# Sliding-window attention and soft-MoE slots on one core: the end of the kernel with direct products of the last weight chunks, and with 5/4 of an expert's second half held back instead

## The chip, the cores and the metric

The kernel runs on one core of one Trainium2 chip. The metric is the device time of one execution in microseconds; lower is better. The median of three runs is shown, and next to it the profile of one execution.

## The reference, and what is computed

Attention over 8 batches x 8 heads x 576 tokens with 64 values a head. Heads 0 to 3 see a window of 32 tokens back, heads 4 to 7 every fourth token of the last 128. Its output, 4608 tokens x 512 values (x), goes into a mixture of experts with 8 experts and 4 slots each:

```python
logits = x @ phi                                  # 4608 x 32
d = np.exp(logits - logits.max(0, keepdims=True))
d /= d.sum(0, keepdims=True) + 1e-09
slot_input = (d.T @ x).reshape(8, 4, 512)
for e in range(8):
    slot_out[e] = np.maximum(slot_input[e] @ w1[e], 0.0) @ w2[e]
c = np.exp(logits - logits.max(1, keepdims=True))
c /= c.sum(1, keepdims=True) + 1e-09
return c @ slot_out.reshape(32, 512)              # 4608 x 512, float32
```

w1 is 8 x 512 x 1024 and w2 is 8 x 1024 x 512. All inputs are float32.

## The kernel before, in words

The program is first a list of operations, each with its engine, a cost, a key and what it reads and writes (`Prog.op`). `Prog.schedule` then plans them: whenever an engine is free, it takes the operation that can start earliest by the costs and the planned landings of loads, and among those within 0.12 us of each other the one with the lowest key. What comes out is a fixed order for each engine. The instructions of SP and POOL keep the order of the program text. `Prog.emit` writes the orders out, with semaphore waits where one engine depends on another. So the orders are settled before the run, and a late operand holds up whatever stands behind it on that engine. In one stretch of the plan (`FILL`) idle time of PE is filled with matmuls whose results nobody reads (L1052, "fillers").

Attention runs in eight units. POOL issues the loads: for each unit q, k and v, and between them the weights, which are cast from float32 to bf16 on the way. PE transposes, makes scores and products, ACT takes exponentials, DVE masks and normalises. For each batch the logits give expT (32 slots spread over 128 rows, times the tokens), and the slot inputs are summed up in a PSUM bank.

After the last unit, with keys from K1 on, comes the stage around the change:

- The slot inputs go through w1 (L814) and a ReLU, give h_sb, and are transposed into hT (L832, L841). `rsum` (L852) sums expT per token, and rtok is its reciprocal.
- `ffn2` (L893) multiplies with w2: for each expert it makes matmuls over chunks cc of the 1024 hidden values, eight chunks an expert, into one of two PSUM banks `sp_[h_]`, one for each half of the 512 output columns ("first half" is columns 0 to 255). Four experts stand side by side in 32 columns of PE each. All calls of `ffn2` are tied into one chain, in the order of the text (`chain`, L891).
- `half(h_, key)` (L939) finishes one half of the columns. The bank is scaled with rcs and becomes so_sb; products of expT with so_sb give the rows of the output, which ACT or DVE scale with rtok on the way from PSUM to SBUF and SP stores (`store`, L920).

The last loads that POOL issues are w25, then, for each half of the columns, expert 6 (512 KB), expert 7 without its last two chunks (384 KB) and the last two chunks alone (128 KB). After them come 15 loads of a few bytes each into a tensor that nothing reads (L782).

The last two chunks of expert 7 (cc 6 and 7) are treated apart. Before `half`, h_sb's columns of those chunks are scaled with m7, which keeps expert 7's rows alone (L863 to L874), and multiplied with the first 512 tokens of expT; that gives two tiles G (L877, evicted on L881 and L884). In `half` so_sb is made without the two chunks. The first two sets of 256 tokens are then the sum of a product with so_sb (L957) and of two *direct* products, of G with the weights of the chunks (L960). Only then does `ffn2((7,), 6, 8, ...)` (L969) complete the bank. All other rows use so_all, a second copy: POOL copies its rows 0 to 95 from so_sb (L944), and the rows 96 to 127, where expert 7 stands, are scaled from the complete bank (L977). The sets o = 2 to 5 of the half use it (L989).

`NAB` is 6: six sets of 256 tokens are stored half by half, 256 KB each. The other 3072 tokens follow when both halves are there, in full rows, as groups of 4, 4, 8 and 8 rows for each partition (L1021 on; products on L1034; evictions by `scaled`, L931 on DVE and L932 on ACT; stores of 1, 1, 2 and 2 MB).

Around the change: `wload` on L773 to L777, `NAB` and `GRP` on L844 and L845, lines 863 to 885, `chain` on L891, `half` from L939, the calls of `ffn2` on L1009 to L1017, and the groups on L1020 and L1021.

Of the kernel before, what the change touches and what calls it, by code (L numbers as in the profile page):

```python
# [302 lines left out]
def bass_dilated_sliding_attn__then__soft_moe_slots_kernel(  # L303
# [46 lines left out]
    so_fin = psA_sb[:].bitcast(BF16)[:, 0:DM]  # L350
    m7 = sb("m7", [128, 1], F32)
# [47 lines left out]
    b_m7 = Buf()  # L399
# [374 lines left out]
    for h_ in range(2):  # L774
        sl = (256 * h_, 256 * h_ + 256)
        wload("w26", ((0, 8) + sl,))
        wload("w27", ((0, 6) + sl, (6, 8) + sl))  # L777

    mk = sb("mk", [15, 136])
    for n_ in range(1, 16):  # L780
        o_ = sum(range(n_))
        op("pool", lambda g, n_=n_, o_=o_: [g.dma_start(mk[0:n_, o_:o_ + n_], moe_w2[7, 0:n_, 0:n_])],  # L782
           cost=0.3, sem=DmaSem(nc, f"s_mark{n_}"), nbytes=1024)
# [60 lines left out]
    NAB = 6  # L844
    GRP = [2] * NAB + [4, 4, 8, 8]  # L845
    rs = tile(psum, 1)

    def rsum(t):
# [13 lines left out]
    op("dve", lambda vv: vv.tensor_reduce(m7[:], ident[:, 100:104], mybir.AxisListType.X, AluOp.add),  # L862
       r=[b_id], w=[b_m7], cost=0.1, key=K1)  # L863
    op("dve", lambda vv: vv.tensor_tensor(m7[:], m7[:], rcs[:], AluOp.mult),
       r=[b_rcs], w=[b_m7], cost=0.1, key=K1)
    h7 = tile(pPT)
    G = [tile(pPT), tile(pPT)]

    def so_all(p0=0, p1=128, sl=slice(0, 512)):
        return so_fin[p0:p1, sl]  # L870
    op("dve", lambda vv: vv.tensor_scalar(sbt(h7)[:, 0:256].rearrange("p (f c) -> p f c", c=2),
                                          h_sb[:].rearrange("p (f c) -> p f c", c=8)[:, :, 6:8],
                                          m7[:, 0:1], None, op0=AluOp.mult),
       r=[b_m7] + b_h, w=[h7], alloc=[h7], cost=0.3, key=K1 + 1.5)  # L874
    for c in range(2):
        gp = tile(psum, 1)
        op("pe", lambda t, c=c, gp=gp: t.matmul(bank(gp)[:, 0:NG], sbt(h7)[:, c:256:2], expT[:, 0:NG],  # L877
                                                start=True, stop=True),
           r=[h7] + b_expT[:2], w=[gp], alloc=[gp, G[c]], cost=0.25, key=K1 + 1.6)
        if c == 0:  # L880
            op("act", lambda ac, gp=gp: ac.activation(sbt(G[0])[:, 0:NG], bank(gp)[:, 0:NG], ACTF.Copy),  # L881
               r=[gp], w=[G[0]], cost=0.6, key=K1 + 1.7)
        else:
            op("dve", lambda vv, gp=gp: vv.tensor_copy(sbt(G[1])[:, 0:NG], bank(gp)[:, 0:NG]),  # L884
               r=[gp], w=[G[1]], cost=0.6, key=K1 + 1.7)

# [4 lines left out]
    chain = []  # L891

    def ffn2(es_, lo, hi_, h_, key, after=()):  # L893
# [3 lines left out]
        def pe(t):  # L897
            for cc in range(lo, hi_):
# [8 lines left out]
               a=[sp_[h_], b_sp[h_]], cost=0.12 * (hi_ - lo), mode="c", key=key, after=chain[-1:] + list(after))  # L907
        chain.append(o)
# [11 lines left out]
    def store(d0, n, ap, ob, key, h_=None):  # L920
        so = DmaSem(nc, f"s_out{d0}_{h_}")
        s_out.append(so)
        dst = out[d0:d0 + 128 * n, :].rearrange("(p j) f -> p j f", j=n)
        if h_ is not None:
            dst, ap = dst[:, :, CH[h_]], ap[:, :, CH[h_]]
        op("sp", lambda e: [e.dma_start(dst, ap)], r=[ob], cost=0.1, sem=so,
           nbytes=262144 * n // (1 if h_ is None else 2), key=key)
# [6 lines left out]
    pb7 = {c0: pb for l2, h2, c0, c1, pb in HOME["w27"][1].parts if l2 == 6}  # L934
    AB = [(256 * o, osts[o // 2][:, 1024 * (o % 2):1024 * (o % 2) + 1024].rearrange(
        "p (j f) -> p j f", j=2), b_ost[o // 2]) for o in range(NAB)]
    b_soah = [[Buf(), Buf()] for _ in range(2)]

    def half(h_, key):  # L939
        sl = CH[h_]  # L940
        eA, eB = (("dve", "act"), ("act", "dve"))[h_]
        xe = op(eA, lambda en: scaled(en, so_sb[:, sl], bank(sp_[h_])[:, 0:256], rcs[:, 0:1]),
           r=[b_sp[h_], b_rcs, sp_[h_]], w=[b_so[h_]], cost=0.45, key=key)
        op("pool", lambda g: g.tensor_copy(so_all(0, 96, sl), so_sb[0:96, sl]), r=[b_so[h_]],  # L944
           w=[b_soah[h_][0]], after=b_psA.ready + b_psA.reads, cost=0.6, key=key + 0.1)
        po = [tile(psum, 1) for _ in range(3)]
        last = [None, None, None]
        for c in (None, 0, 1):
            for o in range(2):
                for j in range(2):  # L950
                    k_ = j if o == 0 else 2
                    d0 = AB[o][0]

                    def pe(t, o=o, j=j, k_=k_, d0=d0, c=c):
                        d_ = bank(po[k_])[:, CH[j] if o else CH[0]]
                        if c is None:
                            return t.matmul(d_, row(d0, 2)[j], so_sb[:, sl],  # L957
                                            start=o == 0 or j == 0, stop=False,
                                            skip_group_check=True)
                        return t.matmul(d_, sbt(G[c])[:, d0 + j:d0 + 256:2], w2v[7][:, 6 + c, sl],  # L960
                                        start=False, stop=c == 1, skip_group_check=True)
                    x = op("pe", pe, r=[b_so[h_]] + b_expT[:2] if c is None else [G[c], pb7[sl.start]],
                           a=[po[k_]], alloc=[po[k_]] if last[k_] is None else [], cost=0.15,
                           key=key + 1 + (0 if c is None else 1 + o) + 0.1 * j,
                           after=[last[k_]] if last[k_] is not None else [])
                    last[k_] = x
                    if c is not None:
                        HOME["w27"][1].reads.append(x)
        ffn2((7,), 6, 8, h_, key + 3.5, after=[xe])  # L969
        d0, ap, prev = AB[0]  # L970
        ob = Buf()
        for j in range(2):
            op(("act", "dve")[j], lambda en, j=j: scaled(
                en, AB[0][1][:, j, sl], bank(po[j])[:, 0:256], rtok[:, j:j + 1]),
               r=[po[j], b_rtok], a=[ob], after=prev, cost=0.4, key=key + 4)
        store(d0, 2, ap, ob, key + 4, h_)
        op(eB, lambda en: scaled(en, so_all(96, 128, sl), bank(sp_[h_])[96:128, 0:256],  # L977
                                 rcs[96:128, 0:1]),
           r=[b_sp[h_], b_rcs, sp_[h_]], w=[b_soah[h_][1]], after=b_psA.ready + b_psA.reads, cost=0.4, key=key + 4.1)
        for o in range(1, NAB):  # L980
            d0, ap, prev = AB[o]
            if o == 1:
                p2 = po[2]
            else:
                p2 = tile(psum, 1)

                def pe(t, d0=d0, p2=p2):
                    for j in range(2):
                        i_ = t.matmul(bank(p2)[:, CH[j]], row(d0, 2)[j], so_all(0, 128, sl),  # L989
                                      start=j == 0, stop=True, skip_group_check=True)  # L990
                    return i_
                op("pe", pe, r=b_soah[h_] + b_expT, w=[p2], alloc=[p2], cost=0.25,
                   key=key + 4 + o)
# [111 lines left out]
```

## Time and profile before

| | us |
|---|---|
| median of 3 runs (179.84, 180.31, 181.1) | 180.31 |
| the profiled execution's own time | 180.75 |
| its span, from first to last instruction | 179.0 |
| PE busy | 136.4 |
| DVE busy | 116.0 |
| ACT busy | 94.1 |
| POOL busy | 47.4 |

HBM is read for 61.94 MB and written for 9.44 MB, 399 GB/s over the span. The queue of POOL's loads (q0) moved 30.94 MB, counted as written in bf16; the stores (q1) 9.50 MB with phi's load. The mean granted clock of PE is 0.972.

In the profile's slices a digit is a share of busy time in tenths, and one slice is a fortieth of the span, 4.5 us. A row of the timeline gives the start, the duration, the engine and line, the operation, what it writes and reads, and in brackets how long the engine was idle before it and what ended that. A row of the windows has the stretch, its length, the busy time of PE, PE's weight loads, DVE, ACT and POOL with their numbers of instructions, the granted clock, the mean number of transfers in progress for each of the 16 DMA engines (DMA share) and the GB/s that they moved.

### The profile page before, as it was taken

How to read it: one execution, taken by the hardware profiler on the slowest of the kernel's cores; microseconds unless marked ns; L12 is line 12 of the kernel's file. 1: busy time of each engine (PE TensorE's matmuls, PEld its weight loads, DVE VectorE, ACT ScalarE, POOL GpSimd, SP SyncE). 2: the span in 40 equal slices, each digit the busy share in tenths (PEclk: the TensorE clock that was granted, in tenths of full speed). 3: DMA queues.
4: the chain of work that ended last, by engine and by line, in shares of the span. 5: the costliest groups of instructions: out<-in, count | busy, mean ns of one | idle time of the engine just before them, and what ended most of it. 6: DMA issues, size and time to landing. Idle time of an engine off the chain costs nothing.

```text
span 179.0 us, 5831 instructions
## 1 busy us (share of the span) xinstructions
PE 136.4 (76%) x2614; PEld 104.3 (58%) x2614; DVE 116.0 (65%) x264; ACT 94.1 (53%) x141; POOL 47.4 (26%) x92
## 2 busy tenths in 40 slices
PE   0019789986988988898998698889999999879000
PEld 0019568865867967676876576865656587533000
DVE  6840297699579589759669669789952233489400
ACT  2004666975765894754895486675330121559300
POOL 7990700600700430620110010023995000000000
PEclk9999999999999999999999999999999999999855
DMA  5999999999999999999999999999999999889996
GB/s 81 192 216 212 216 214 212 222 214 212 219 210 210 217 214 217 208 226 207 220 208 220 211 216 222 212 211 223 212 211 213 194 198 118 251 293 396 421 458 293
DMA packets 13384, 40.81 MB, mean 228 GB/s; under 512 B 2352, under 2 KB 9520, under 8 KB 9520
## 3 DMA queue, kind: packets, MB, share of 16 engines
q0 software_dynamic: 8992, 30.94, 86.9%
q1 hardware_dynamic: 4368, 9.50, 14.1%
q8 instruction: 20, 0.33, 0.7%
q14 instruction: 4, 0.03, 0.0%
HBM read 61.94 MB, written 9.44 MB: 399 GB/s over the span
## 4 chain that ended last, share of the span: by engine, by line
PE 47%; DVE 28%; ACT 9%; DMA 5%; issue 3%; POOL 1%; DVEq 0%; POOLq 0%
DVE XB L651 9%; PE ps L549 7%; DVE PT L601 7%; DMA stg<-in_v_dram 5%; PE ps L544 5%; PE ps L695 5%; PE ps L611 5%; ACT PT L593 4%; PE ps L668 4%; DVE VN L616 4%; PE ps L586 3%; DVE WD L931 3%; PE ps L1052 3%; PE ps L901 3%; ACT TT L568 3%
## 5 line engine op out<-in xcount | busy, mean ns | idle before, releaser
L568 ACT ACTIVATE TT<-ps 128x864 f32<-128x864 f32 x32 | 28.6, 894 | 31.6 <-PE ps L549 22.5
L593 ACT ACTIVATE PT<-ps 128x768 bf16<-128x768 f32 x48 | 37.0, 813 | 8.4 <-PE ps L586 8.1
L549 PE MATMUL ps<-ident,stg 96*64 96x96 bf16 x576 | 18.3, 226 | 16.4 <-DMA stg<-in_v_dram 12.9
L651 DVE TENSOR_TENSOR XB<-ps,RV 96x768 bf16<-96x768 f32 x32 | 30.3, 948 | 0.7
L549 PEld LDWEIGHTS ps<-ident,stg 96*64 96x64 bf16 x576 | 16.0, 124 | 18.0 <-DMA stg<-in_v_dram 12.9
L616 DVE COPY VN<-ps 128x768 bf16<-128x768 bf16 x32 | 17.6, 548 | 11.8 <-PE ps L611 11.8
L415 POOL DMA_DIRECT2D stg<-in_q_dram x16 | 8.4, 533 | 46.1 <-PE ps L549 23.8
L640 PE MATMUL ps<-VN,PT 128*128 128x65 bf16 x384 | 18.1, 195 | 2.3 <-DVE PT L601 0.9
L611 PE MATMUL ps<-ident,TT 128*128 128x128 bf16 x192 | 17.7, 232 | 1.6 <-issue 0.9
L640 PEld LDWEIGHTS ps<-VN,PT 128*128 128x128 bf16 x384 | 14.8, 99 | 4.8 <-DVE PT L601 1.7
L586 PE MATMUL ps<-TT 64*128 64x96 bf16 x384 | 15.8, 211 | 2.0 <-ACT TT L568 1.0
L680 DVE COPY XT<-ps 128x576 bf16<-128x576 bf16 x17 | 10.1, 596 | 10.4 <-PE ps L668 10.3
L611 PEld LDWEIGHTS ps<-ident,TT 128*128 128x128 bf16 x192 | 11.8, 103 | 5.9 <-issue 2.3
L544 PE MATMUL ps<-ident,stg 96*128 96x96 bf16 x288 | 14.9, 206 | 0.2
L668 PE MATMUL ps<-ident,XB 96*128 96x96 bf16 x192 | 12.7, 207 | 2.5 <-DVE XB L651 2.2
L932 ACT ACTIVATE WD<-ps,rtok 128x256 f32<-128x256 f32 (+1 forms) x18 | 8.7, 591 | 9.5 <-PE ps L960 6.7
L586 PEld LDWEIGHTS ps<-TT 64*128 64x128 bf16 x384 | 10.1, 97 | 6.1 <-issue 1.7
L601 DVE TENSOR_TENSOR PT<-PT,mask_d 128x768 bf16<-128x768 bf16 x24 | 13.0, 544 | 0.9 <-ACT PT L593 0.4
L544 PEld LDWEIGHTS ps<-ident,stg 96*128 96x128 bf16 x288 | 13.0, 98 | 0.5 <-ACT PT L593 0.3
L448 POOL DMA_DIRECT2D stg<-in_moe_w_dram x6 | 3.2, 533 | 38.1 <-PE ps L544 25.5
L601 DVE TENSOR_TENSOR PT<-PT,mask_p 128x768 bf16<-128x768 bf16 x24 | 12.7, 541 | 0.4 <-ACT PT L593 0.4
L668 PEld LDWEIGHTS ps<-ident,XB 96*128 96x128 bf16 x192 | 9.5, 98 | 5.1 <-DVE XB L651 4.2
(95 smaller groups left out, 202.3 us busy)
## 6 DMA issues: line engine op xcount, KB each, us to landing
WD<-in_moe_w_dram POOLq DMA_DIRECT2D x7, 1024.0 KB, 26.2
stg<-in_moe_w_dram POOLq DMA_DIRECT2D x6, 1024.0 KB, 21.3
stg<-in_q_dram POOLq DMA_DIRECT2D x16, 288.0 KB, 16.2
stg<-in_k_dram POOLq DMA_DIRECT2D x16, 288.0 KB, 18.1
stg<-in_v_dram POOLq DMA_DIRECT2D x16, 288.0 KB, 20.1
out_dram<-WD SPq DMA_DIRECT2D x12, 256.0 KB, 3.4
out_dram<-WD SPq DMA_DIRECT2D x2, 1024.0 KB, 5.5
out_dram<-WD SPq DMA_DIRECT2D x1, 2048.0 KB, 8.8
```

What stands on the lines that cost most here:

```text
L544: i_ = t.transpose(bankb2(pt, a)[:, 96 * kk:96 * kk + 96], two[:, j // 2, c, :], ident[0:96, 0:96])
L549: i_ = t.transpose(bankb2(pt, a)[64 * hx:64 * hx + 64, 96 * kk:96 * kk + 96], src[:, hx, c, :], ident[0:96, 0:96])
L568: return ac.activation(d, sv, ACTF.Copy)
L586: i_ = t.matmul(pair(sc)[:, hx, QB * x:QB * x + QB], win(u, 1, h01, blk_, bpar)[64 * hx:64 * hx + 64], win(u, 0, h01, blk_, bpar)[64 * hx: ...
L593: op("act", lambda ac: ac.activation(sbt(pt)[:, 0:768].rearrange("p (x n) -> p x n", x=2), pair(sc)[:, :, 0:384], ACTF.Exp, scale=SCALE), ...
L601: return dv.tensor_tensor(p_, p_, m.unsqueeze(1).to_broadcast([128, 2, 384]), AluOp.mult)
L611: i_ = t.transpose(bankb(pv)[:, 128 * m:128 * m + 128], win(u, 2, h01, m, bpar), ident[:, :])
L616: op("dve", lambda dv: dv.tensor_copy(sbt(vn)[:, :, :, 0:64], bankb(pv)[:, 0:768].rearrange("p (m x d) -> p m x d", m=6, x=2)), r=[pv], w= ...
L640: i_ = t.matmul(pair(po)[:, bk, 65 * po_:65 * po_ + 65], sbt(pts[i])[:, o_:o_ + 128], sbt(vn)[:, m, half, 0:65], start=True, stop=True)
L651: op("dve", lambda dv: dv.tensor_tensor(sbt(xb)[:].rearrange("p m (x h d) -> p h x m d", x=2, h=2)[:, h01], pv()[:, :, :, 0:64], sbt(rv)[: ...
L668: i_ = t.transpose(bankb(px)[:, QB * m:QB * m + QB], sbt(xb)[:, m, 128 * x:128 * x + 128], ident[0:QB, 0:QB])
L680: return en.tensor_copy(d, s_)
```

## The change

The last two chunks of expert 7 are no longer treated apart. m7, the scaled copy of h, G and its evictions, the direct products, so_all and POOL's copy are gone; every row of the output is made from so_sb, which is complete.

The loads are cut otherwise: of expert 6, chunks 0 to 5 come in full rows (both halves, 768 KB) and chunks 6 and 7 for the first half (128 KB), then expert 7's first half in two pieces of 256 KB. What is left, two chunks of expert 6 and all eight of expert 7 for the second half, comes last.

`ffn2`'s chain is now one for each half. The experts 4 and 5 are cut into chunks 0 to 3 and 4 to 7, and expert 6's chunks 0 to 5 of both halves go among the early products. The second half's rest (expert 6's chunks 6 and 7, expert 7) depends, by `after=mm0`, on all the token products of the first half. No other operand of theirs needs that.

In `half`, the first set of 256 tokens is evicted and stored in two pieces of 128 KB, one for each row of a partition. `NAB` is 5, so five sets are stored by halves, and a fifth group, of two rows a partition (512 KB), joins those of the full rows. The tensor of the 15 small loads has another name.

```diff
-    for h_ in range(2):
-        sl = (256 * h_, 256 * h_ + 256)
-        wload("w26", ((0, 8) + sl,))
-        wload("w27", ((0, 6) + sl, (6, 8) + sl))
+    wload("w26", ((0, 6, 0, 512), (6, 8, 0, 256)))
+    wload("w27", ((0, 4, 0, 256), (4, 8, 0, 256)))
+    wload("w26", ((6, 8, 256, 512),))
+    wload("w27", ((0, 4, 256, 512), (4, 8, 256, 512)))
...
-    NAB = 6
-    GRP = [2] * NAB + [4, 4, 8, 8]
+    NAB = 5
+    GRP = [2] * NAB + [2, 4, 4, 8, 8]
...
-    op("dve", lambda vv: vv.tensor_scalar(sbt(h7)[:, 0:256].rearrange("p (f c) -> p f c", c=2),
-                                          h_sb[:].rearrange("p (f c) -> p f c", c=8)[:, :, 6:8],
-                                          m7[:, 0:1], None, op0=AluOp.mult),
...
-        op("pe", lambda t, c=c, gp=gp: t.matmul(bank(gp)[:, 0:NG], sbt(h7)[:, c:256:2], expT[:, 0:NG],
-                                                start=True, stop=True),
...
-    chain = []
+    chain = [[], []]
...
-               a=[sp_[h_], b_sp[h_]], cost=0.12 * (hi_ - lo), mode="c", key=key, after=chain[-1:] + list(after))
-        chain.append(o)
+               a=[sp_[h_], b_sp[h_]], cost=0.12 * (hi_ - lo), mode="c", key=key, after=chain[h_][-1:] + list(after))
+        chain[h_].append(o)
...
-        op("pool", lambda g: g.tensor_copy(so_all(0, 96, sl), so_sb[0:96, sl]), r=[b_so[h_]],
-           w=[b_soah[h_][0]], after=b_psA.ready + b_psA.reads, cost=0.6, key=key + 0.1)
...
+            if o == 0:
                 for j in range(2):
...
+                    p1 = tile(psum, 1)
+                    mm.append(op("pe", lambda t, j=j, p1=p1: t.matmul(
+                        bank(p1)[:, 0:256], row(0, 2)[j], so_sb[:, sl], start=True, stop=True),
+                        r=[b_so[h_]] + b_expT, w=[p1], alloc=[p1], cost=0.15, key=k2))
+                    ob = Buf()
+                    op((e1, e0)[j], lambda en, j=j, ap=ap, p1=p1: scaled(
+                        en, ap[:, j, sl], bank(p1)[:, 0:256], rtok[:, j:j + 1]),
+                       r=[p1, b_rtok], a=[ob], after=prev, cost=0.4, key=k2)
+                    store(d0, 2, ap, ob, k2, h_, j)
+                continue
...
-    ffn2((6,), 0, 8, 0, K1 + 10)
-    ffn2((7,), 0, 6, 0, K1 + 11)
-    half(0, K1 + 20)
-    ffn2((6,), 0, 8, 1, K1 + 30)
-    ffn2((7,), 0, 6, 1, K1 + 31)
+    for h_ in range(2):
+        k_ = K1 + 2 + 0.5 * h_
+        ffn2((0, 1, 2, 3), 0, 8, h_, k_)
+        ffn2((4, 5), 0, 4, h_, k_ + 2)
+        ffn2((4, 5), 4, 8, h_, k_ + 2.1)
+        ffn2((6,), 0, 6, h_, k_ + 4)
+    ffn2((6,), 6, 8, 0, K1 + 10)
+    ffn2((7,), 0, 4, 0, K1 + 11)
+    ffn2((7,), 4, 8, 0, K1 + 12)
+    mm0 = half(0, K1 + 20)
+    ffn2((6,), 6, 8, 1, K1 + 30, after=mm0)
+    ffn2((7,), 0, 4, 1, K1 + 31)
+    ffn2((7,), 4, 8, 1, K1 + 32)
     half(1, K1 + 40)
...
-    for i, (n, hs) in enumerate(((4, (3,)), (4, (4,)), (8, (5, 6)), (8, (7, 8)))):
-        if hs[-1] == 8:
+    for i, (n, hs) in enumerate(((2, (2,)), (4, (3,)), (4, (4,)), (8, (5, 6)), (8, (7, 8)))):
+        if n == 2:
+            ap = osts[hs[0]][:, 1024:2048]
+        elif hs[-1] == 8:
```

## The prediction

> **What bounds the kernel now.** I read the page's slices first, then the DMA issues, then windows and timelines of the last 35 us. The page shows where the engines stop and the transfers do not:
>
> ```profile
> span 179.0 us, 5831 instructions
> ...
> PE   0019789986988988898998698889999999879000
> ...
> DMA  5999999999999999999999999999999999889996
> GB/s 81 192 216 212 216 214 212 222 214 212 219 210 210 217 214 217 208 226 207 220 208 220 211 216 222 212 211 223 212 211 213 194 198 118 251 293 396 421 458 293
> ```
>
> One slice is 4.5 us. The DMA engines are busy all along, at about 212 GB/s while loads are cast to bf16, with a dip to 118 in slice 34, and at 396 to 458 GB/s in the stores at the end. PE is idle in the last three slices: the end is set by stores. So I ask when the stores begin and where their stream is thin. Windows over that stage (last column GB/s, before it the DMA share):
>
> ```profile
> 147.00:148.50 1.50, 1.50 (x36) 1.41 (x31) 0.00 (x0) 0.00 (x0) 0.00 (x0) 1.00 1.46 198
> ...
> 152.00:152.80 0.80, 0.80 (x9) 0.53 (x8) 0.18 (x2) 0.26 (x1) 0.00 (x0) 1.00 0.24 23
> ```
>
> ```profile
> 152.80:156.00 3.20, 2.37 (x22) 1.71 (x20) 1.27 (x2) 2.08 (x6) 0.40 (x1) 1.00 0.96 279
> 156.00:159.00 3.00, 2.01 (x17) 1.22 (x14) 2.40 (x5) 0.90 (x3) 0.00 (x0) 1.00 1.04 351
> 159.00:160.50 1.50, 1.44 (x8) 0.60 (x6) 1.50 (x3) 1.50 (x5) 0.00 (x0) 1.00 0.54 184
> 160.50:163.00 2.50, 2.50 (x11) 0.88 (x10) 2.50 (x5) 2.50 (x6) 0.00 (x0) 1.00 1.04 344
> 163.00:178.10 15.10, 2.48 (x9) 0.78 (x8) 4.41 (x7) 3.94 (x7) 0.00 (x0) 0.70 1.00 421
> ```
>
> Loads run out by 152.8, and stores flow from there to 178.1 without a stop. Half-row stores (12 of 256 KB, 3.15 MB) reach 351 GB/s, the full-row stores (6.29 MB) 421. Two stretches are thin: 152.8 to 156.0 loses 3.2 x (351 - 279) / 351 = 0.66 us, and 159.0 to 160.5 loses 1.5 x (351 - 184) / 351 = 0.71 us. The timeline has their cause:
>
> ```profile
> 149.41 0.48 DVE L931 TENSOR_SCALAR so_sb<-ps,rcs 128x256 bf16<-128x256 f32 x1 [4.03 <-PE ps L901]
> ...
> 151.55 0.62 SPq L926 DMA_DIRECT2D out_dram<-WD  x1
> ```
>
> ```profile
> 154.99 0.61 PE L957 MATMUL ps<-so_sb,expT 128*128 128x256 bf16 x4 [0.83 <-ACT so_sb L932]
> 155.44 1.04 PE L960 MATMUL ps<-TT,PT 128*128 128x256 bf16 x8
> 156.40 0.39 PE L901 MATMUL ps<-TT,hT 128*32 128x256 bf16 x2
> 157.78 1.05 PE L989 MATMUL ps<-psA_sb,expT 128*128 128x256 bf16 x8 [0.99 <-DVE psA_sb L931]
> ```
>
> ```profile
> 157.23 0.56 SPq L926 DMA_DIRECT2D out_dram<-WD  x1
> ```
>
> ```profile
> 158.93 0.53 SPq L926 DMA_DIRECT2D out_dram<-WD  x1
> ```
>
> First bytes leave at 152.8, 1.25 us after the first issue at 151.55. SP issues nothing between 157.79 and 158.93, because the second half's complete slot output (L931, psA_sb) is late: the direct products and the last two expert products are in front of it, and then DVE is still evicting. 1.15 us behind that hole lies the 184 GB/s stretch.
>
> **The change, part by part.** All times are those of the profiled execution (180.75 us, span 179.0). The median of the runs shown is 180.31, 0.44 lower; I make the sum on the former and take the difference from the median.
>
> 1. Loads. From issue to landing, the seven last loads took 18.5 us (1024 KB, issued 123.83), 20.6 (512, 124.35), 21.8 (384, 125.24), 21.7 (128, 126.06), 23.6 (512, 126.75), 24.7 (384, 127.64) and 24.6 (128, 128.45), so they landed at 142.3, 145.0, 147.0, 147.7, 150.3, 152.3 and 153.1. A 1024 KB load of whole rows takes 4.85 us behind another (137.5 to 142.3), half-row loads of 512 KB 2.6, of 128 KB 0.7, and in between I put 256 KB at 1.35. The new list (768 whole rows, 128, 256, 256, then for the second half 128, 256, 256) lands at 146.0, 146.7, 148.0, 149.4, 150.1, 151.5 and 152.8. The last landing gains 0.3 us; but all of the first half is in at 149.4, where the old one needed only the 147.0 landing for its first product. POOL issues eight loads for seven, 0.7 to 0.9 us more before its 15 marker loads; the 20 us of queue between issue and landing hide that, and without that cover it would cost those 0.9 us.
>
> 2. First half on PE. Removed: the scaled copy of h (0.34 on DVE), two G products (0.59 PE), their evictions (0.60 ACT, 0.69 DVE). They lie beside the experts' products or where PE ran fillers; they give nothing. Before, the last product of the first half's 110-matmul run starts at 149.10. Now two more of expert 7 and six of expert 6's second half are ahead of it: 8 x 0.109 = 0.87 (8 matmuls of L960 take 1.04, of which 0.27 is the last one's own), so 149.97. The load would allow 149.4 + 0.1 + 3 x 0.109 = 149.8; PE is just the later. Then, by the old distances: 0.31 to the scaling on DVE, 0.48 for it, 0.07 to the token product, 0.31 to the eviction (ACT, no direct products between: 8 x 0.109 saved), 0.47 for it, 0.04 to SP: 151.65, against 151.55. That is +0.1 us. Bounds: -0.1 if the pieces of experts 6 and 7 overlap on PE as they do now, +0.6 if the last load lands by the 128 KB pace throughout (4 x 0.1) and PE adds a switch of 0.21. I take +0.1.
>
> 3. First-half stores. The first 256 KB go as two of 128 KB. SP took 0.53 to 0.63 us for 256 rows and 0.33 for 128: two times 0.33, as before. All later sets no longer wait for the eviction of the last expert's rows and L989 behind it (152.35). ACT: 0.47, then two sets of 2 x 0.39 to 153.2; DVE 0.48, then 2 x 0.65 to 153.1. SP: 151.65, 151.98, 152.4, 153.05, 153.7, 154.3, free at 154.9. Before, the third issue was at 153.50 and the engines were thin at 154 to 155. Gain: of the 0.66 us lost, the part with idle engines, about 0.27 (255 GB/s in that us); the rest was slow with engines full and I leave it. Bounds 0 and 0.66.
>
> 4. Second half. Its last products wait behind the ten token products (to 150.83 + 10 x 0.109 = 151.9) and for the load at 152.8. Queued behind that wait on PE are only the second half and the full rows. Last product 153.25, ACT (free at 153.2) scales from 153.55 to 154.05, token product 154.1, eviction 154.4 to 154.9, SP at 154.95, where it was 156.59. Six issues later (two of 0.33, four of 0.63) SP is at 158.2. By 156.2, when the second half's first bytes can leave, the engines have moved some 1.0 of the 1.31 MB issued: 0.8 us of stock. The 159.0 hole closes: -0.71. Bounds -0.71 and -0.3, the latter if SP's 128-row issues cost 0.6 each and the stock runs out briefly.
>
> 5. Full rows. Removed: POOL's copies (0.39, 0.40) and the 32-row scalings (0.47, 0.49). Five row groups instead of four; 0.52 MB go at 4 KB per partition instead of 1 KB: between nothing and 0.52/0.351 - 0.52/0.421 = 0.25 us, I take 0.13, the middle. 26 row tiles on ACT and DVE at 0.65 each engine's 13 end near 165.2, last issue 165.3 instead of 167.48. It gives nothing: the engines then still have some 5 MB, 12 us, to store.
>
> Sum: +0.1 - 0.27 - 0.71 - 0.13 = -1.0 us, 180.31 to 179.3.
>
> A rule that speaks against part 3. The row: stores issued at 154.74 and 155.41 both took 3.6 us to land, 0.67 apart, so what is fixed in a store overlaps its neighbours. The Trainium skill, page "DMA: Bandwidth & Descriptors", section "Anatomy of one DMA — SWDGE (gpsimd) path", fits a fixed 2.0 us per transfer, and the section "Bandwidth" advises 1 MiB or more at a time. There will be 17 stores for 16; were the fixed part paid in the stream, the sum would be -1.0 + 2.0 = +1.0, 181.3. That fit is of the other queue's transfers one by one; these rows do not pay it.
>
> **Rivals.**
> A. As summed, 179.3; its own range, from the bounds of the parts: 178.6 to 180.6.
> B. The hole moves instead of closing: SP's small issues or the slower first stretch keep the engines waiting, so parts 3 and 5 give nothing and part 4 only 0.3: +0.1 - 0.3 = -0.2, 180.1. For it: with 0.67 us per 256 KB SP is only just faster than the 0.75 that the engines take. Against it: the 0.8 us of stock in part 4.
> C. Slower: the first half's last load is late. Loads end when their slowest engine is through, and the DMA share falls from 1.46 to 0.24 between 147 and 152.8, so the engines drain unevenly. Each us that expert 7's second piece lands after 149.4 delays every store by one; at 150.4 the gain is gone. If it landed with the second half's, at 152.8, that is +3.4 - 1.0 = +2.4, 182.7. Against it: the old pieces landed in order, at even steps.
> D. All bounds at their good ends: -0.1 - 0.66 - 0.71 - 0.25 = -1.7, 178.6, or a little under with a good draw of runs.
>
> **How the numbers follow.** Chances: A 0.55, B 0.22, C 0.10, D 0.13. The time is A's, 179.3. One per cent, 1.8 us, is about what a measurement of this kernel can tell from no change. Faster by more than that (under 178.5) is most of D and a corner of A: 0.12; slower (over 182.1) most of C and some unforeseen wait: 0.10; the rest 0.78. For 8 in 10 the range takes A, B and D and the small delays of C: 178.3 to 181.0.
>
> **What would show it.** Right: first store issue within 0.2 us of 151.65, second half's first near 155, no window under 340 GB/s from 156 on, last issue near 165. Wrong: a first store after 152.6 (part 2), SP idle between 155 and 158.5 or a dip there (part 4), 128-row issues of 0.6 us (part 3), a last landing of loads after 153.1 (part 1).

## The result, and the profile after

The changed kernel takes 179.54 us (median of 17 runs, 179.05 to 181.75), the kernel before 180.06 in 17 runs beside it (179.46 to 181.3). The ratio is 0.9955, with a 95% interval of 0.9935 to 0.9975: some 0.8 us less, between 0.45 and 1.2, which is within 1%. 179.3 had been predicted. The profiled execution took 179.56 us with a span of 177.8, where that of before took 180.75 with 179.0. These 1.2 us are more than the medians differ by (0.52); a section below takes this up.

The slices of the page after, 4.4 us each:

```profile
span 177.8 us, 5774 instructions
...
PE   0009768989988788897987898798999996796000
...
DMA  5999999999999999999999999999999999799996
GB/s 71 201 209 220 205 222 212 220 207 216 218 205 217 219 213 216 212 217 214 214 217 210 214 219 216 212 219 217 210 221 214 209 192 143 200 350 409 448 435 295
```

The shape is as before: loads at 212 GB/s, a dip of one or two slices (143 and 200 now, 118 and 251 before), then stores up to the end, now a few slices of 350 GB/s and more. The same windows over the last stage as were shown of before, with the one ahead of them:

```profile
151.40:152.80 1.40, 1.27 (x13) 0.71 (x11) 1.40 (x3) 1.40 (x5) 0.00 (x0) 1.00 0.52 90
152.80:156.00 3.20, 2.28 (x16) 1.44 (x18) 1.56 (x4) 2.09 (x6) 0.00 (x0) 1.00 0.90 279
156.00:159.00 3.00, 2.97 (x12) 1.11 (x12) 3.00 (x6) 3.00 (x7) 0.00 (x0) 1.00 1.05 351
159.00:160.50 1.50, 1.42 (x5) 0.42 (x5) 1.50 (x4) 1.50 (x4) 0.00 (x0) 1.00 1.01 348
160.50:163.00 2.50, 2.38 (x8) 0.82 (x8) 2.50 (x5) 2.50 (x6) 0.00 (x0) 1.00 1.08 432
163.00:177.10 14.10, 0.12 (x1) 0.00 (x0) 1.98 (x4) 1.16 (x3) 0.00 (x0) 0.65 0.98 412
```

Read the last column. The hole of 159.0 to 160.5 is filled (348 GB/s where it was 184), and 160.5 to 163.0 runs at the pace of full rows (432 where it was 344). The first stretch, 152.8 to 156.0, runs at the same pace, 279 GB/s in both. But the stores begin before it: in 151.4 to 152.8, where before had only the last loads, 60 GB/s more are moved. That window before:

```profile
151.40:152.80 1.40, 1.40 (x16) 1.07 (x16) 0.78 (x3) 0.47 (x1) 0.00 (x0) 1.00 0.32 30
```

PE's timeline around the end of the loads:

```profile
148.37 0.61 PE L873 MATMUL ps<-TT,hT 128*32 128x256 bf16 x4 [0.35 <-DMA TT<-in_moe_w_dram]
149.67 0.61 PE L873 MATMUL ps<-TT,hT 128*32 128x256 bf16 x4 [0.69 <-DMA TT<-in_moe_w_dram]
150.86 0.39 PE L923 MATMUL ps<-so_sb,expT 128*128 128x256 bf16 x2 [0.58 <-DVE so_sb L905]
...
153.09 0.61 PE L873 MATMUL ps<-TT,hT 128*32 128x256 bf16 x4 [0.42 <-DMA TT<-in_moe_w_dram]
154.27 0.39 PE L923 MATMUL ps<-so_sb,expT 128*128 128x256 bf16 x2 [0.57 <-ACT so_sb L906]
```

Each group of last products (L873) waits for a load; the brackets name it. The first half is complete when the load that landed at 149.62 is in, the second when that of 153.05 is. The scalings and SP's issues (L900) follow:

```profile
150.32 0.48 DVE L905 TENSOR_SCALAR so_sb<-ps,rcs 128x256 bf16<-128x256 f32 x1 [7.90 <-PE ps L873]
```

```profile
153.74 0.47 ACT L906 ACTIVATE so_sb<-ps,rcs 128x256 bf16<-128x256 f32 x1 [0.62 <-PE ps L873]
```

```profile
152.55 0.62 SPq L900 DMA_DIRECT2D out_dram<-WD  x1
```

```profile
155.21 0.62 SPq L900 DMA_DIRECT2D out_dram<-WD  x1
```

155.21 is the second half's first store, which was issued at 156.59 before. The third store of the first half leaves at 152.55 (153.50 before). SP issued at 151.68, 152.07, 152.55 and then every 0.5 to 0.8 us to 160.27, with no gap over 0.76.

### The profile page after: what moved, and what is told of

It is laid out like the page before. It is cut to its first block, busy times and chain, and to the rows that moved or that the text cites. A ratio compares the mean times of both kernels' runs of the same rounds, so it can differ in the third digit from the quotient of the medians.

```text
span 177.8 us, 5774 instructions
## 1 busy us (share of the span) xinstructions
PE 131.8 (74%) x2589; PEld 100.3 (56%) x2594; DVE 113.0 (64%) x258; ACT 93.1 (52%) x140; POOL 46.8 (26%) x91
## 4 chain that ended last, share of the span: by engine, by line
PE 26%; DMA 25%; DVE 22%; POOL 8%; ACT 7%; issue 3%; DVEq 0%; POOLq 0%
DMA TT<-in_moe_w_dram 15%; DMA stg<-in_v_dram 10%; DVE XB L648 7%; DVE PT L598 5%; POOL stg L412 4%; ACT PT L590 4%; PE ps L546 4%; PE ps L608 4%; PE ps L692 4%; PE ps L541 4%; DVE WD L905 3%; DVE VN L613 3%; PE ps L665 3%; PE ps L583 3%; POOL TT L445 3%
## 5 line engine op out<-in xcount | busy, mean ns | idle before, releaser
L546 PE MATMUL ps<-ident,stg 96*64 96x96 bf16 x576 | 17.3, 220 | 16.5 <-DMA stg<-in_v_dram 13.7
L546 PEld LDWEIGHTS ps<-ident,stg 96*64 96x64 bf16 x576 | 15.1, 120 | 18.1 <-DMA stg<-in_v_dram 13.8
L637 PE MATMUL ps<-VN,PT 128*128 128x65 bf16 x384 | 17.6, 194 | 2.2 <-DVE PT L598 0.9
L608 PE MATMUL ps<-ident,TT 128*128 128x128 bf16 x192 | 16.3, 221 | 1.9 <-issue 1.1
L637 PEld LDWEIGHTS ps<-VN,PT 128*128 128x128 bf16 x384 | 14.3, 98 | 4.9 <-DVE PT L598 1.6
L583 PE MATMUL ps<-TT 64*128 64x96 bf16 x384 | 15.2, 204 | 1.8 <-ACT TT L565 1.0
L608 PEld LDWEIGHTS ps<-ident,TT 128*128 128x128 bf16 x192 | 10.9, 98 | 5.8 <-issue 2.5
L583 PEld LDWEIGHTS ps<-TT 64*128 64x128 bf16 x384 | 9.6, 94 | 5.7 <-ACT TT L565 1.1
```

What stands on the lines that cost most here:

```text
L546: i_ = t.transpose(bankb2(pt, a)[64 * hx:64 * hx + 64, 96 * kk:96 * kk + 96], src[:, hx, c, :], ident[0:96, 0:96])
L583: i_ = t.matmul(pair(sc)[:, hx, QB * x:QB * x + QB], win(u, 1, h01, blk_, bpar)[64 * hx:64 * hx + 64], win(u, 0, h01, blk_, bpar)[64 * hx: ...
L608: i_ = t.transpose(bankb(pv)[:, 128 * m:128 * m + 128], win(u, 2, h01, m, bpar), ident[:, :])
L637: i_ = t.matmul(pair(po)[:, bk, 65 * po_:65 * po_ + 65], sbt(pts[i])[:, o_:o_ + 128], sbt(vn)[:, m, half, 0:65], start=True, stop=True)
```

## The experiments

All times are against the kernel before on the same chip. The groups of experiments ran on different chips, so kernels of different groups are compared by their ratios or by events of their profiles. "span" and the times of events are those of one profiled execution. The pace of the changed kernel by the same measure is 0.9955. My theory was that the end is set by the bytes that the stores have moved, so that a thin stretch costs what is missing in it, and that the change gains by closing the hole at 159. The rivals were that the order on PE does not matter, that the sooner first full rows make the gain, and that the first store alone decides.

**1. The binding taken away.**

```diff
-    ffn2((6,), 6, 8, 1, K1 + 30, after=mm0)
+    ffn2((6,), 6, 8, 1, K1 + 30)
```

> The changed kernel without the dependency of the second half's late products on the first half's token products. In the written order PE then has all ten late products ahead of the first token product. Theory (the end is the first store plus the stream of stores): the first half's rows wait for the last landing, near 153.0 instead of 149.6, so the first store is issued near 155 instead of 151.7; some 0.5 us of the thin early stretch comes back, so about +2.7 us on the changed kernel, 182.3, ratio to before 1.012. Rival (the dependency is idle, the gain came from the removed work alone): same time as the changed kernel, 0.9955.

Measured: 182.54 us, ratio 1.0155 (1.0139 to 1.0172), span 180.8. PE and the bytes of the stretch:

```profile
151.28 1.04 PE L873 MATMUL ps<-TT,hT 128*32 128x256 bf16 x4 [0.95 <-DMA TT<-in_moe_w_dram]
152.63 1.03 PE L873 MATMUL ps<-TT,hT 128*32 128x256 bf16 x4 [0.32 <-DMA TT<-in_moe_w_dram]
153.60 0.61 PE L923 MATMUL ps<-so_sb,expT 128*128 128x256 bf16 x2
```

```profile
152.80:156.00 3.20, 3.20 (x16) 2.02 (x15) 1.23 (x3) 2.15 (x6) 0.00 (x0) 0.50 0.14 48
```

so_sb's first half was scaled from 149.91, yet its token products (L923) begin at 153.60, after the second half's products, which had to wait for the last load. The first store leaves at 154.57, 2.9 us later than after, and the end is 3.0 later. The granted clock is 0.50 in this window (1.00 after): 4 late products take 1.03 us instead of 0.61, and the first token products 0.61 instead of 0.39, so some 0.4 to 0.6 of the delay is the clock and the rest the order. The binding is worth some 3 us (3.6 by the ratios), and the gain of the change exists only with it.

**2. Six sets by halves, as before.**

```diff
-    NAB = 5
-    GRP = [2] * NAB + [2, 4, 4, 8, 8]
+    NAB = 6
+    GRP = [2] * NAB + [4, 4, 8, 8]
...
-    for i, (n, hs) in enumerate(((2, (2,)), (4, (3,)), (4, (4,)), (8, (5, 6)), (8, (7, 8)))):
+    for i, (n, hs) in enumerate(((4, (3,)), (4, (4,)), (8, (5, 6)), (8, (7, 8)))):
```

> The changed kernel with six sets stored by halves instead of five, so the group of two full rows is gone. Theory: 0.52 MB go at some 351 instead of 412 GB/s, +0.2 us, ratio 0.9967, and no hole near 159. Rival (the gain is from fewer and larger stores): all of the gain goes, ratio 1.000.

Measured: 179.55 us, 0.9978 (0.9964 to 0.9992), span 177.9. There is no hole at 159 either (352 GB/s). The fifth group is not what closes it. The median is 0.35 us under that of before, where the change gave 0.52; the difference of the ratios, 0.0023, is 0.4 us with intervals that overlap, so the predicted 0.13 is not contradicted and not shown.

**3. The first half later by six matmuls.** Six extra matmuls write columns that nobody reads, after the last product of the first half.

```diff
+            for x in range(idle):
+                i_ = t.matmul(bank(sp_[h_])[96:128, 256:512], hT[:, 1, 7, 3, :],
+                              w2v[7][:, 7, CH[h_]], start=True, stop=True, skip_group_check=True)
...
-    ffn2((7,), 4, 8, 0, K1 + 12)
+    ffn2((7,), 4, 8, 0, K1 + 12, idle=6)
```

> The changed kernel with six matmuls of 0.109 us, into unused columns of the bank, behind the last product of each kind for the first half: its scaling starts 0.65 us later. Theory: stores start 0.65 later and the stream ends 0.65 later, ratio 0.9991. Rival (the stream has slack at its start, SP or the thin stretch sets the pace): less than 0.2, ratio 0.996.

Measured: 180.17 us, 1.001 (0.9991 to 1.0029), span 178.4. The first store leaves at 152.30 (+0.62), the last landing is at 177.96 (+0.60). In the profile the first half is on the path, one to one. The ratios differ by 1.0 us, with intervals wide enough for 0.6.

**4. The second half later by twelve.** The same loop, after the second half's last product.

```diff
-    ffn2((7,), 4, 8, 1, K1 + 32)
+    ffn2((7,), 4, 8, 1, K1 + 32, idle=12)
```

> The changed kernel with twelve matmuls of 0.109 us behind the last product of the second half: its scaling starts 1.31 us later. Theory: the stores of the first half are a stock of some 0.6 us, the rest is a hole in the stream, +0.7, ratio 0.9994. Rival 1 (no stock, the second half is on the path): +1.3, ratio 1.003. Rival 2 (the stock covers all of it, the closed hole was not what paid): 0, ratio 0.9955.

Measured: 180.42 us, 1.003 (0.9997 to 1.0064), span 178.8, which is +1.0 for 1.31 added. The second half's first store leaves at 156.56 (+1.35), and 156 to 159 falls from 351 to 291 GB/s, a loss of 3.0 x 60 / 351 = 0.5 us. The other 0.5 came otherwise: in this execution PE's expert products began 2.6 us later than after and the first store left at 152.18 (+0.5). Taken apart so, 1.35 us of delay in the second half cost 0.5; the stock in front of it would hide the rest, about 0.8. Since two delays were mixed in one profile, this is a rough figure, and the runs do not bear it out: by the ratios the delay costs 1.35 us (0.6 to 2.1), and 1.003 is the ratio that was expected if there were no stock at all. How much of such a delay the stock hides stays open.

**5. The first store in one piece.**

```diff
+                ob = Buf()
...
-                    ob = Buf()
...
-                    store(d0, 2, ap, ob, k2, h_, j)
+                store(d0, 2, ap, ob, k2, h_)
```

> The changed kernel with the first set of each half stored as one piece of 256 KB instead of two of 128. The first issue is 0.4 us later (152.07), the third store of before 0.1 later. Theory (the early stretch is set by when the second set's bytes come, not by the first bytes): +0.1 us, ratio 0.996. Rival (each first byte counts): +0.4, ratio 0.998.

Measured: 179.45 us, 0.9976 (0.9959 to 0.9992), span 177.8, last landing 177.35 against 177.36. The first issue moved from 151.68 to 151.82 and the first bytes from 152.6 to 153.1, but then they flow at 297 GB/s instead of 279 in 152.8 to 156.0. In the profile the split buys nothing; the ratio is 0.4 us worse than that of the change, with intervals that overlap. Fifteen stores take the time of seventeen: the fixed 2.0 us per transfer of the Trainium skill, page "DMA: Bandwidth & Descriptors", section "Anatomy of one DMA — SWDGE (gpsimd) path", which the prediction weighed and left out, is not paid in this stream.

**6. All of expert 6 held back too (8/4 of an expert per half for 5/4).** The first half then needs less before its end.

```diff
-    wload("w26", ((0, 6, 0, 512), (6, 8, 0, 256)))
+    wload("w26", ((0, 8, 0, 256),))
...
-    wload("w26", ((6, 8, 256, 512),))
+    wload("w26", ((0, 8, 256, 512),))
...
-        ffn2((6,), 0, 6, h_, k_ + 4)
-    ffn2((6,), 6, 8, 0, K1 + 10)
+    ffn2((6,), 0, 8, 0, K1 + 10)
...
-    ffn2((6,), 6, 8, 1, K1 + 30, after=mm0)
+    ffn2((6,), 0, 8, 1, K1 + 30, after=mm0)
```

> The changed kernel with 8/4 of an expert's second half held back instead of 5/4: all of experts 6 and 7, the loads cut by halves, all behind the first half's token products. The first half is loaded near 147.9 instead of 149.6, so the first store is issued near 150 and its bytes use DMA engines that have run out of loads (share 0.5 to 0.7 in 150 to 152.8); the second half still waits for the last landing, 153.0 or up to 0.8 later where stores and loads share an engine. Theory: -0.7 from the earlier bytes and -0.3 from the thin stretch, but the 1.31 MB of the first half then run out before the second half comes, a hole of 0.6 to 1.4: -0.4 to +0.4 on the changed kernel, ratio 0.993 to 0.998, with a hole near 156. Rival (first store sets the end one to one): -1.5, ratio 0.987.

Measured: 179.46 us, 0.9968 (0.9956 to 0.998), span 177.8. The first store leaves at 149.92, 1.76 us earlier, and the end is the same (177.37). The windows of this kernel:

```profile
151.40:152.80 1.40, 0.63 (x5) 0.30 (x4) 0.00 (x0) 0.00 (x0) 0.00 (x0) 1.00 1.17 187
152.80:156.00 3.20, 2.27 (x16) 1.44 (x18) 1.34 (x3) 1.77 (x5) 0.00 (x0) 1.00 0.86 260
156.00:159.00 3.00, 2.97 (x12) 1.13 (x12) 3.00 (x6) 3.00 (x7) 0.00 (x0) 1.00 0.97 328
```

After has 90, 279 and 351 GB/s there. So 1.4 x 97 = 0.136 MB are moved sooner, and 3.2 x 19 + 3.0 x 23 = 0.130 MB are lost again in a new hole at 155 to 158 (176, 313 and 320 GB/s by the us): the stores of the first half run out before the second half's first, which cannot leave before 155.11 (last load). The hole does not explain all of it, though: between 148.5 and 151.4 this kernel had moved 0.14 MB more than after, and it keeps a lead. From 176 on it has 66 KB left to store, after 262 KB, and both end together. Nothing is left of the 1.76 us; experiment 7 shows more of why.

**7. The same with seven sets by halves,** to fill that hole; beside the edits of 6:

```diff
-    NAB = 5
-    GRP = [2] * NAB + [2, 4, 4, 8, 8]
+    NAB = 7
+    GRP = [2] * NAB + [2, 4, 8, 8]
...
-    for i, (n, hs) in enumerate(((2, (2,)), (4, (3,)), (4, (4,)), (8, (5, 6)), (8, (7, 8)))):
+    for i, (n, hs) in enumerate(((2, (3,)), (4, (4,)), (8, (5, 6)), (8, (7, 8)))):
```

> As e4, but seven sets of 256 tokens stored by halves instead of five: 1.83 MB of the first half bridge the wait for the second. Theory: no hole near 156; 0.52 MB more per two sets in short packets costs 0.2 to 0.3; -0.6 on the changed kernel, ratio 0.992. Rival (stores that run beside the last loads delay these by as much, nothing is won): +0.3, ratio 0.997.

Measured: 179.98 us, 0.9999 (0.9985 to 1.0012), span 178.3. The hole is gone, no stretch from 152.8 to 176 is under 300 GB/s, and still the end is 0.5 us later than after (0.8 by the ratios). Here my theory of bytes fails. The last windows of this kernel and of after:

```profile
175.00:176.00 1.00, 0.00 (x0) 0.00 (x0) 0.00 (x0) 0.00 (x0) 0.00 (x0) 0.50 0.73 311
176.00:177.00 1.00, 0.00 (x0) 0.00 (x0) 0.00 (x0) 0.00 (x0) 0.00 (x0) 0.50 0.27 115
```

```profile
175.00:176.00 1.00, 0.00 (x0) 0.00 (x0) 0.00 (x0) 0.00 (x0) 0.00 (x0) 0.50 1.00 426
176.00:177.00 1.00, 0.00 (x0) 0.00 (x0) 0.00 (x0) 0.00 (x0) 0.00 (x0) 0.50 0.62 262
```

Look at the DMA share, the number before the last. At 175 this kernel has some 0.43 MB left to store and after 0.69, so it is ahead in bytes; but from 176 to 177 only 27% of its engines' time is used, where after has 62%: a few engines carry its end. The trace says so directly: it has 16 landings for each transfer, and those of the last store come from 176.05 to 177.85 us here, but from 177.15 to 177.36 after. The loads end unevenly too: the 16 landings of the last load come from 149.22 to 153.35 here, and from 148.88 to 153.05 after. My reading is that what is moved early is moved by engines that are through with their loads early, and that the end waits for the others. That the engines late at the end are those which ended their loads last is inferred; no run isolates it. The expectation's rival, that stores beside the last loads delay these, is not excluded: the last load landed 0.3 later than after.

**8. Four sets by halves.**

```diff
-    NAB = 5
-    GRP = [2] * NAB + [2, 4, 4, 8, 8]
+    NAB = 4
+    GRP = [2] * NAB + [4, 4, 4, 8, 8]
...
-    for i, (n, hs) in enumerate(((2, (2,)), (4, (3,)), (4, (4,)), (8, (5, 6)), (8, (7, 8)))):
+    for i, (n, hs) in enumerate(((4, (2,)), (4, (3,)), (4, (4,)), (8, (5, 6)), (8, (7, 8)))):
```

> The changed kernel with four sets stored by halves instead of five; the next group has four rows a partition. Theory: 0.52 MB more go in long packets, -0.2, and the 1.05 MB of the first half run out near 156.2, about when the second half's bytes come: 0 to -0.2 on the changed kernel, ratio 0.9945 to 0.9955. Rival (five sets are just enough): a hole of 0.7 us, ratio 0.998.

Measured: 179.24 us, 0.9954 (0.9929 to 0.9979), span 177.2. It has the lowest median of all, 0.3 us under after's, but the ratio is after's and the intervals cover each other: it beats the kernel before and is not shown to beat the change. Its shorter span does not show it either: in that execution the loads were early, the last one landing at 152.50 for 153.05.

**9. Both: eight held back, four sets.** The edits of 6 and 8 together:

```diff
-    wload("w26", ((0, 6, 0, 512), (6, 8, 0, 256)))
+    wload("w26", ((0, 8, 0, 256),))
...
-    NAB = 5
-    GRP = [2] * NAB + [2, 4, 4, 8, 8]
+    NAB = 4
+    GRP = [2] * NAB + [4, 4, 4, 8, 8]
```

> As e4 (8/4 held back) with four sets instead of five. In the run with seven sets only three to five of the 16 DMA engines were still storing in the last 1.5 us. Theory: the end is set by the engines that finish their loads last, and a hole on the others costs nothing, so long packets pay: -0.25 on e4, ratio 0.9945 to 0.996. Rival (the stream as a whole sets the end): the first half's bytes run out 0.75 us earlier and the hole costs it, +0.5 on e4, ratio 0.9995.

Measured: 179.51 us, 0.9978 (0.9966 to 0.999), span 178.0. PE's expert products began late in the profiled execution (145.61), so its first store left at 151.59 and the profile says nothing of the question. The ratio lies between the two expectations; inconclusive.

**10. The kernel before once more.** Unchanged, for a second profile: did the experts' products, which begin at 145.01 before and 142.97 after, belong to the change?

> The kernel before, unchanged, profiled once more. In the profile of before PE began the experts' second products at 145.0; in those of the changed kernel and its variants it began between 141.4 and 145.5, with the same order of work up to there. Theory: that start wanders from one execution to the next and before the change it set the first store (151.55). If PE begins near 143 here, the first store is issued near 150, and the hole in front of the second half is longer, since that half waits for the load at 153.0 all the same: span 178.0 to 178.7. Rival (145.0 is this kernel's own start, and the change moved it): start at 145.0 again, first store 151.55, span 179.0.

Measured: one run, 181.65 us, span 179.9. Products from 145.92 (+0.91), first store 152.46 (+0.91), last landing 179.43 (+0.89). Neither expectation held, as it was later yet. But between these two executions of the kernel before the start of the products carries through to the end one to one.

**11. Before, and 12. after, with PE warmed.** Both with 100 matmuls of the identity with itself on PE while the first loads are under way.

```diff
+    wt = tile(psum, 1)
+
+    def pe_w(t):
+        for _ in range(100):
+            i_ = t.matmul(bank(wt)[:, 0:128], ident[:, :], ident[:, :], start=True, stop=True)
+        return i_
+    op("pe", pe_w, r=[b_id], w=[wt], alloc=[wt], cost=6.0, key=-1)
```

> The kernel before with 100 matmuls on the identity, whose results nobody reads, on PE while it waits for the first loads. In both profiles of before the first unit's groups ran slow to about 25 us (six transposes 0.82 us) and in that of the changed kernel only to about 17 (0.51), so PE came 2 to 3 us later to the end. Theory: with PE warm the experts' products start near 142.5, the first store is issued near 150, the second half still waits for the load at 153.0 and what is behind it, so the hole in front of it grows: 0.3 to 0.8 us gained on before, ratio 0.996 to 0.998. Rival 1 (first store sets the end alone): -1.6, ratio 0.991. Rival 2 (the start of PE does not matter): 1.000.

> The changed kernel with the same 100 matmuls at the start. Theory: its first half waits for the load at 149.6, not for PE, so an earlier PE gives nothing: first store at 151.7, ratio 0.9955. Rival (PE's start sets the first store here too): first store near 150, ratio 0.988.

Measured, before with it: 179.94 us, 1.0012 (0.9985 to 1.004), span 178.1. Products from 142.66, first store 150.15 (1.4 earlier than in the first profile of before), end 177.62 (0.9 earlier): the second half's first store (155.89) gained only 0.7. In the runs this is no gain. The profile of before that I had predicted from was a late one, so the usual execution of before is probably like this already; no profile of it shows that.

Measured, after with it: 180.75 us, 1.0045 (1.0029 to 1.0061), span 179.3. That is slower, and both expectations were wrong. Windows of this kernel and of after:

```profile
152.00:153.00 1.00, 0.57 (x5) 0.30 (x4) 0.37 (x1) 0.47 (x2) 0.00 (x0) 1.00 0.66 87
153.00:154.00 1.00, 0.43 (x5) 0.33 (x5) 0.04 (x1) 0.47 (x1) 0.00 (x0) 1.00 0.07 16
```

```profile
152.00:153.00 1.00, 0.67 (x8) 0.31 (x6) 1.00 (x2) 1.00 (x4) 0.00 (x0) 1.00 0.70 131
153.00:154.00 1.00, 0.61 (x4) 0.30 (x4) 0.02 (x1) 0.38 (x2) 0.00 (x0) 1.00 0.59 179
```

The stores stop between 153 and 154 (share 0.07). The first two, 128 KB each, left at 151.04 and 151.43, with so_sb earlier by 0.6 than after; they landed only at 155.07 and 155.59, and the third was not issued before 154.01, though ACT and DVE had evicted its rows by 152.5. SP waits there for nothing that the profile shows. In the record a transfer of instructions, 16 KB, is open from 151.50 to 153.58, 2.1 us where such a transfer took 0.9 to 1.0 in before and after. The two coincide; that the one causes the other is not shown, and why 100 more instructions on PE would bring it there stays open.

## Why the prediction was right, and where it was not

The time was right (179.3 against 179.54), and in the two profiles the chief mechanism came as forecast: the second half's first store leaves 1.4 us earlier, and the hole behind it closes. That the two times lie so close is in part luck. A gain of 1.0 us was forecast, and the medians differ by 0.52 (0.8 by the ratio); the base, 180.31 from three runs, lay 0.25 over the median of 17, and the two misses offset each other in part. By the steps of the sum:

1. **Loads.** Right within 0.25 us. The last pieces landed at 146.27, 146.94, 148.33, 149.62, 150.30, 151.65 and 153.05, where 146.0, 146.7, 148.0, 149.4, 150.1, 151.5 and 152.8 had been worked out. The distances between landings (0.7 for 128 KB, 1.3 to 1.4 for 256 KB) were the right measure.
2. **First half on PE.** The time was right, 151.68 for 151.65, and the reason wrong. I had put PE just behind the load. In the profiled execution PE came two microseconds earlier and waited 0.69 us for the load of 149.62, which was 0.2 later than I had it. The two errors cancel.
3. **First-half stores.** The way failed, the size was about met. The step gave 0.27 us for the third issue being at 152.4 rather than 153.50. The issue was at 152.55, and the stretch still moves 279 GB/s. What I left out is that the bytes of a store of 256 rows start some 1.25 us after its issue: nearly all of the first 256 KB were moved by 153.5, and those of the third came at about 153.8. The thin place went from 154.5 to 153.6 and stayed. What was gained instead lies ahead of the stretch: the first bytes came at 152.53 for 152.81, though the first issue was 0.13 later, and 1.4 x (90 - 30) = 0.084 MB more were moved before 152.8, some 0.2 us at 421 GB/s. Steps 2 and 3 together had -0.17. Experiment 5 shows the same from its other side: without the split the stream begins later and is denser, and ends at the same time.
4. **Second half.** Right: 155.21 for 154.95 and the hole closed, 184 to 348 GB/s, 1.5 x (348 - 184) / 351 = 0.70 us for 0.71. The 0.26 us are the load's, which landed at 153.05 for 152.8, but SP would not have come much sooner: the issue ahead of it began at 154.54, and such issues are some 0.67 us apart. Its issues of 128 rows, 0.39 apart instead of 0.33, cost nothing. The stock can be read off: by 156.0 the first half's stores had moved 0.08 + 3.2 x 0.279 = 0.97 of their 1.31 MB, so that nearly 1 us of work was left, where 0.8 had been put. What it hides when the second half is late is not settled (experiment 4).
5. **Full rows.** The direction is right and the size not settled: 160.5 to 163.0 runs at 432 GB/s for 344, while experiment 2 with six sets lost 0.1 us in the span and 0.4 by the ratios. That the last issue is early (165.06, predicted 165.3) gives nothing, as was said.

Between the last landings of the two profiles lie 1.18 us: 0.70 from the hole, 0.2 from the stores before 152.8, and at most the 0.25 of step 5. If step 5 gave its most, next to nothing is left over.

This accounts for that pair, and the profile of before in it is a late one. The only early one that the kernel before has is experiment 11, with its 100 matmuls more and a median like that of before. Its window at 159:

```profile
159.00:160.50 1.50, 1.50 (x8) 0.63 (x6) 1.50 (x4) 1.50 (x4) 0.00 (x0) 1.00 0.94 319
```

There the hole at 159 is nearly gone without the change (319 GB/s for 184; 152.8 to 156.0 is thinner instead, 225), and the last landing is only 0.26 us behind that of after (177.62 for 177.36). So the 0.70 us of step 4 belong to the late execution. What makes up the 0.5 to 0.8 us between the medians is not shown.

**The phase of PE.** The work of attention is the same in both kernels, but the experts' products began anywhere between 141.4 and 145.9 in the 14 profiles. The difference is there at 20 us already. The same transposes of before and of after:

```profile
20.29 0.82 PE L611 MATMUL ps<-ident,TT 128*128 128x128 bf16 x6
```

```profile
19.49 0.51 PE L608 MATMUL ps<-ident,TT 128*128 128x128 bf16 x6
```

Six take 0.82 us in one and 0.51 in the other; in before the slow pace lasts until about 25 us. The windows give a granted clock of 1.00 up to there in both, but the first clock that the traces record, full speed, is at 25.67 us before and at 17.15 after, and there the pace changes. Experiment 11 has records from 9 us on, and there the row itself shows the lower clock (0.58) while its transposes take 0.82:

```profile
16.00:19.00 3.00, 0.73 (x26) 0.60 (x26) 0.00 (x0) 1.43 (x2) 0.80 (x2) 1.00 1.07 221
19.00:22.00 3.00, 3.00 (x42) 2.13 (x40) 2.04 (x4) 2.21 (x3) 2.72 (x6) 0.58 1.02 211
```

So the slow pace is read as the lower clock. In two profiles of the kernel before a late PE moves the first store and the end one to one (145.01 and 145.92: first store 151.55 and 152.46, last landing 178.54 and 179.43). An early one does less: in experiment 11 (142.66) the products come 2.35 us sooner, the first store 1.4 and the end 0.9. In the changed kernel the first half waits for its load, so in the four kernels with the same first half and the usual start (after and experiments 2, 5 and 8: 142.4 to 143.3) the first store left at 151.1 to 151.8, as its load landed; only the late start of experiment 4 showed (152.18). So the sum was made against a profile that was late by chance: its 180.75 us lie 0.7 over the median of 17 runs. The Trainium skill, page "TensorE: Matmul & The Clock Gate", section "What's actually happening", says that the clock comes up after about 3.4 us of sustained work, counted in windows that run freely, so that the point of the change varies by 500 ns. After agrees with it: PE's first work is at 13.04 and the full clock at 17.15. Before does not: from 12.89 to 25.67 are 12.8 us, though PE was busy 5.86 of the 6 us from 13 to 19. The measurement decides, and the reason is open. By the same section the clock falls after an idle window of the same length. With the 100 matmuls of experiment 11 the transposes ran at 0.57 at 19.2 us and at 0.82 again from 20.1, after two gaps of only 1.4 and 1.0 us, with PE busy 0.73 of the 3 us from 16 to 19: pauses well under a window were enough here.

**The rivals.** B (the hole moves) came true only for the thin place of step 3. C (the first half's load late) came true by 0.2 us out of the 1.0 that it needed; experiment 3 has its price, one for one, in the profile. D was out of reach: it needed 0.66 us of step 3, which gave about 0.2.

## What to carry to other kernels

Where stores set the end, look for the thin stretches in windows of a microsecond or so and name the wait behind each one: between the two profiles closing the hole gained what the windows said, and moving the first store 1.76 us forward gained nothing while the next half could not follow. Bytes moved early did not count here where a few engines carried the end (experiments 6 and 7); look how many engines still work in the last microseconds, not at the sum of bytes alone. When a prediction is built on one profiled execution, see how that execution stands to the median, and ask what in it may have been late by chance: the hole that this change was to close is nearly gone in experiment 11, where the kernel before is not late.

## What the hardware showed that I had not expected

- From issue to first bytes a store took 0.85 us with 128 rows (151.68 to 152.53) and 1.25 with 256 (151.82 to 153.07 in experiment 5), and 256 KB were moved before the third store's bytes came. Splitting the first store brought the first bytes forward and opened a gap behind them; the end was the same.
- The engines' end is uneven, and the share alone does not tell the end: from 176 to 177 the engines are 62% busy after, 16% in experiment 6, which ends at the same time, and 27% in experiment 7, which ends 0.5 us later.
- Work on PE that nobody needs is not always free, even where PE is idle: with 100 matmuls at 5 us the changed kernel takes 1.6 us more by the ratios (1.0045 against 0.9955), and its profile has a stop of the stores whose cause is open. The kernel before takes no more with them (1.0012).
- In experiment 1 the granted clock was 0.50 from 151.4 to 156, after PE had been busy only 0.73 of the 1.5 us from 148.5 to 150.0 and 0.45 of the 1.4 us from 150.0 to 151.4. From 152.8 on PE was busy throughout, and the clock stayed at 0.50 up to 156. Four products took 1.03 us for 0.61.
